# Threshold attention with an ELU feed-forward block: where SP's queue issues the loads of the next queries, of the tenth pair's values and of the next keys

## The chip, the cores and the metric

The kernel runs on one core of one Trainium2 chip. The metric is the device time of one execution in microseconds. Before the change, three runs took 1256.55, 1258.20 and 1259.09 us; the median is 1258.2 us.

## What is computed

```python
# q, k, v: (8 batches, 8 heads, 576 positions, 64); tau a number; all float32
scores = q @ k.transpose(0, 1, 3, 2) / 8
thresh = scores.max(-1, keepdims=True) - tau
scores = where(scores >= thresh, scores, -1e9)
scores = scores - scores.max(-1, keepdims=True)
attn = exp(scores); attn = attn / (attn.sum(-1, keepdims=True) + 1e-9)
y = attn @ v                                  # (8, 8, 576, 64)
x = y.transpose(0, 2, 1, 3).reshape(4608, 512)
h = x @ w_in                                  # w_in (512, 2048)
g = where(h > 0, h, exp(minimum(h, 0)) - 1)
out = g @ w_out                               # w_out (2048, 512), out (4608, 512)
```

## The kernel before

**Pairs.** Attention is worked off by pairs of heads, numbered from 0 to 31 (`NP`); four pairs make one batch. The code calls a pair `pr`, and its 576 positions are cut into four blocks of 128 and a rest of 64, the steps 0 to 3 and `NC`. The queries of a pair come in four DMAs of 72 KB into the buffer `qm`, the keys in four into `km`, the values in four (`vm` and `vd`, one of each for each head): `load` (L526) and `load_v` (L553). VectorE then transposes queries and keys in squares of 32 (`prep_q`, L577 to L579, and `prep_k`, L588 to L592); a scaling of the queries on POOL or ScalarE and a copy of keys follow.

**Two ways of ordering.** The first nine pairs are laid out by `early_tasks` (L1313): each step is a task with a time at which it is due, with corrections from the table `MOVED`, and with tasks that must come ahead of it; they are issued in the order of their times. From pair 9 on (`JOINED`, L1179), the tenth and the first *wide* one, a loop (L2133) writes out the order. It keeps a clock of its own, which each piece of TensorE work moves on, and an agenda: `at(t, f, key)` (L1673) puts f in at time t, moved by the table's entry for the stage and the key. The first wide pair has the stage "j", the others "s" and "f" in turn. These clocks only set in which order each engine's instructions are issued. On the chip every engine, and SP with its DMA issues, works its list in order and waits on semaphores. The DMAs of SP's queue take turns on eight semaphores, so that an issue also waits for the landing of the one eight before it.

**One wide pair.** `tail_step` (L1964) does the scores of the rest of 64 and the values of the pair two before. Then come two halves: `wide_step` (L1986) does the scores of two blocks for both heads, and maximum, exponential, mask, sum and reciprocal follow on VectorE, ScalarE and POOL. After each half's scores stand 14 quarters of feed-forward products on TensorE (`ffn_quarters`, L1930) for a batch that is done: either first products (`first_product`, L1703, seven products to a unit, the sums of blocks of w_in coming in by DMA as `sw`) or second rounds (`second_round`, L1834, with `t` coming in from `wout_sums`). The feed-forward products rotate through three banks of TensorE's result memory; a bank is written again when its readers have done, among them the adds of VectorE at L1746 and L1873. The two kinds fill pairs in turn: from pair 10 on, even pairs hold second rounds and odd pairs first products.

**The loads of a wide pair, before.** All go through SP. Seven microseconds (of the agenda's clock) after the pair's start come its own values (L2152), which the tail two pairs later reads. In the first half, behind `prep_q` of the next pair, come the next pair's keys (L2008); in the second half, behind `prep_k`, the queries of the pair after the next (L2006). Queries and keys share one buffer, `qm`, from here on (`shared`). So the queries of pair n+1 are issued in the second half of pair n-1, and `prep_q(n+1)` reads them in the first half of pair n. Between these loads SP issues the stores of the transposed weights (`there`, L886 and L898), their fetches (`wTa`, `wTb`, L906 and L910), the rests (`xtail`, L1072), the loads of sums (L1255, L1285) and the stores of results (L1148).

**The first wide pair, before.** The values of pair 9, the queries of pair 10 and the keys of pair 10 are loads of `early_tasks` (L1454 to L1462); the queries of pair 11 are loaded in pair 9's second half.

Of the kernel before, what the change touches and what calls it, by code (L numbers as in the profile page):

```python
# [368 lines left out]
def kernel(  # L369
# [806 lines left out]
    NP = B * NPAIR  # L1176
    NB = NC + 1
    per_seq = NPAIR * NB
    JOINED = (2 * NPAIR + 1)  # L1179
# [133 lines left out]
    def early_tasks():  # L1313
# [104 lines left out]
        for pr in range(1, NPAIR + 6):  # L1418
            old = ("sc", number[pr - 2, NC]) if pr > 1 else None
            own = pr < NPAIR  # L1420
            for x, name in enumerate("qk"):
                n = 2 * pr - 2 + x if own else number[pr - 1, 2 + x]
                k, late_ = kind(n), n >= LATE
                sooner = 2.0 * (n >= SWITCH)
                if pr in QK_PE:
                    tn = turned.setdefault(pr, {})

                    def run_turn(pr=pr, name=name, tn=tn):
                        room_for("t", lambda: do(("prep", name, pr)))
                        tn[name] = turn_blocks(pr, name)  # L1430

                    task(("turnqk", name, pr), begin[n] + (6.7 - sooner if late_ else 1.6), None, run_turn, ("load", name, pr))
                    task(("prep", name, pr), begin[n] + (6.8 - sooner if late_ else 1.7), f"p{name}{k}",
                         lambda pr=pr, name=name, tn=tn: copy_blocks(pr, name, tn[name]), ("turnqk", name, pr), None if own else old,
                         ("prep", "q", pr) if x else None)
                    if x:
                        def run_last(pr=pr, tn=tn):
                            room_for("t", lambda: do(("last", pr)))
                            tn["last"] = turn_last(pr)

                        task(("turnlast", pr), begin[n] + (6.7 - sooner if late_ else 1.6), None, run_last, ("load", "q", pr), ("load", "k", pr))
                        task(("last", pr), begin[n] + (6.8 - sooner if late_ else 1.7), None, lambda pr=pr, tn=tn: copy_last(pr, tn["last"]),
                             ("turnlast", pr), ("prep", "q", pr), ("prep", "k", pr))
                        made["scale", pr] = made["last", pr]
                else:
                    task(("prep", name, pr), begin[n] + (6.8 - sooner if late_ else 1.7), f"p{name}{k}",
                         lambda pr=pr, f=(prep_q, prep_k)[x]: f(pr), ("load", name, pr), None if own else old, ("prep", "q", pr) if x else None)
                if not x and pr not in QK_PE:
                    task(("scale", pr), begin[n] + (6.85 - sooner if late_ else 1.75), f"sq{k}", lambda pr=pr: scale_q(pr), ("prep", "q", pr))
                m = number[pr, 2] if own and not x else n  # L1450
                task(("copy", name, pr), begin[m] + (6.9 - sooner if late_ else 1.8), f"c{name}{kind(m)}",
                     lambda pr=pr, f=(copy_q, copy_k)[x]: f(pr), ("prep", name, pr), ("scale", pr) if not x or pr in QK_PE else None,
                     old if not x else None)
            for x, name in enumerate("qk"):  # L1454
                n = 2 * pr - 1 + x if own else number[pr - 1, 3 + x]
                late_ = n >= LATE
                task(("load", name, pr + 1), begin[n] + (7.0 if late_ else -1.0 if own else 4.6), f"l{name}{kind(n)}",
                     lambda pr=pr, name=name: load(pr + 1, (name + "m",)), ("prep", name, pr), ("last", pr) if pr in QK_PE else None)
            if pr > 1:
                n = 2 * pr - 3 if own else number[pr - 1, 3]  # L1460
                task(("v", pr), begin[n] + (7.1 if n >= LATE else 4.7), f"lv{kind(n)}", lambda pr=pr: load(pr, ("v",)),
                     ("load", "q", pr), None if own else ("val", pr - 2, 1))  # L1462
# [3 lines left out]
        for i, (n, x) in enumerate(slots):  # L1466
            late_, k, t = n >= LATE, f"{kind(n)}{x}", begin[n]
# [48 lines left out]
        for n in range(MIDDLE):  # L1516
            pr, i = steps[n]
# [143 lines left out]
    with tc.manual_schedule():  # L1661
# [11 lines left out]
        def at(t, f, key=None):  # L1673
            if key and stage[0]:
                t += MOVED.get(stage[0] + key, 0.0)
            serial[0] += 1
            heapq.heappush(agenda, (t, serial[0], f))
# [308 lines left out]
        def wide_step(pr, half):  # L1986
            t = clock[0]
            on_pe(2.15, lambda: wide_scores(pr, half))
            e = t + 2.15
            for s in range(2):  # L1990
                i = 2 * half + s
                at(e + 1.55 + 1.5 * s, lambda i=i: wide_bounds(pr, i), f"bound{i}")
                for h in range(2):
                    k = 2 * s + (h ^ s)
                    at(e + 0.75 * k, lambda i=i, h=h: wide_max(pr, i, h), f"max{i}{h}")
                    at(e + (1.6, 3.0, 4.7, 5.6)[k], lambda i=i, h=h: wide_exp(pr, i, h), f"exp{i}{h}")
                    at(e + (3.0, 4.3, 6.5, 6.9)[k], lambda i=i, h=h: wide_mask(pr, i, h), f"mask{i}{h}")
                finish_of(pr, i, e + (5.1, 7.8)[s], e + (8.4, 10.5)[s])
            if pr + 1 < NP:
                at(e + 5.2, lambda: (prep_k if half else prep_q)(pr + 1), f"prep{half}")  # L2000
                if not half:
                    at(e + 6.1, lambda: scale_q(pr + 1), "qscale")
                if half:
                    at(e + 6.1, lambda: copy_k(pr + 1), "kcopy")
                    if pr + 2 < NP:
                        at(e + 6.1, lambda: load(pr + 2, ("qm",), True), "loadq")  # L2006
                elif pr > JOINED:
                    at(e + 6.1, lambda: load(pr + 1, ("km",), True), "loadk")  # L2008
            extras(e + 0.3, e + 1.2, e + 4.2, e + 10.4, e + 12.0)
# [123 lines left out]
        for pr in range(JOINED, NP + 2):  # L2133
            t = clock[0]
            b = pr // NPAIR
            stage[:] = "j" if pr == JOINED else "sf"[pr % 2], BEFORE if pr == JOINED else 0, 0
            if pr == JOINED + 1:
                ges.append((raw.tile([P, S // T, T], FP32, name="km").rearrange("p j d -> p (j d)")[:, : 2 * CT], lambda: None))
            if pr == JOINED:
                for x, i in enumerate((NB - 2, NB - 1)):  # L2140
                    at(t + 6.0 + 3.0 * x, lambda pr=pr, i=i: fetch(pr - 1, i), f"fetch{x}")
                for x in range(3):
                    at(t + 7.0 + 6.0 * x, lambda x=x: nc.sync.dma_start(wout_sums[0, x], out_sums[x].rearrange("p u n -> p (u n)")), f"w{x}")
            elif pr <= NP:
                for x, i in enumerate((NC, 0, 1, 2, 3)):
                    at(t + 6.0 + 3.8 * x, lambda pr=pr, i=i: fetch(pr - 1, i), f"fetch{i}")
            if pr == NP:
                at(t + 12.0, split_begin)
                for x in range(8):
                    at(t + 1.0 + 1.9 * x, lambda: run_extra(max(0.9, extra[0][0])) if extra else None)  # L2150
            if JOINED < pr < NP:
                at(t + 7.0, lambda pr=pr: load(pr, ("v",)), "v" if stage[0] == "j" else None)  # L2152
            tail_step(pr)
            v_end = clock[0]
            if pr % NPAIR == 1 and pr < NP + 1:
                if b > 2:
                    xs = [late["first"].tile([P, 2, CT], FP32, name=f"x{x}") for x in range(3)]
                    jobs = sums_x(b - 1, xs)
                    at(t + 0.9, jobs[1])
                    for x, when in ((0, 0.6), (2, 1.3), (3, 4.0), (4, 4.7)):  # L2160
                        at(v_end + when, jobs[x])
                if pr > JOINED:
                    group(b - 1)
            if pr == NP + 1:
                break
            extras(t + 0.6, t + 2.8)
            begin, first_half = next(iter(SPLIT)) if pr == JOINED else (0, HALF_QUARTERS)
            ffn_quarters(begin - BEFORE if pr == JOINED else begin)
            for half in range(2):
                if pr < NP:  # L2170
                    wide_step(pr, half)
                ffn_quarters(2 * HALF_QUARTERS - begin - first_half if half else first_half)
# [225 lines left out]
```

## Time and profile before

| what | value |
|---|---|
| median of three runs | 1258.2 us |
| the profiled execution, its own time | 1257.49 us |
| its span, first to last instruction | 1255.7 us |
| granted TensorE clock, mean | 0.999 |
| TensorE matmuls busy | 1243.7 us, 99% |
| VectorE busy | 1039.8 us, 83% |
| POOL busy | 727.8 us, 58% |
| ScalarE busy | 635.4 us, 51% |
| DMA | 245.74 MB, mean 196 GB/s |
| DMA packets | 323871, of them under 512 B 207536 |

Busy times are of one execution, which the hardware profiler took down. An instruction's row has its start, its duration, engine, line of the kernel and the tiles that it writes and reads (out<-in). SPq rows are DMA issues: the duration is that of the issue, and the time to landing stands in another view. A busy TensorE is one with a matmul in flight.

### The profile page before, as it was taken

What the parts mean: (1) busy time and instruction counts of PE and PEld (TensorE: products, weight loads), DVE (VectorE), ACT (ScalarE), POOL (GpSimd) and SP (SyncE); (2) the same over time, 40 slices, a digit from 0 to 9 for tenths busy, and PEclk for the clock granted to TensorE, in tenths of its full rate; (3) what the DMA queues carried; (4) which work ended last, traced back from release to release, by engine and by line L of the source; (5) the groups of instructions that cost most, each with busy time, mean ns of one, the idle gap of its engine ahead of it and who ended that gap; (6) DMA issues with size and microseconds to landing.
All of it is one profiled execution on the core that took longest, in us unless ns stands there. A gap on an engine that the chain in (4) does not pass through costs nothing.

```text
span 1255.7 us, 21110 instructions
## 1 busy us (share of the span) xinstructions
PE 1243.7 (99%) x6596; PEld 956.7 (76%) x6596; DVE 1039.8 (83%) x2195; ACT 635.4 (51%) x1334; POOL 727.8 (58%) x1064
## 2 busy tenths in 40 slices
PE   8999999999999999999999999999999999999998
PEld 6675575477888787888778788878788887788886
DVE  7888777789898978998889889898889886776983
ACT  7899776664453526253534445352625352465330
POOL 5778655687575748676576747584767655122000
PEclk9999999999999999999999999999999999999999
DMA  7467788998989898898989988999889785000001
GB/s 150 147 172 184 171 246 228 262 271 219 237 227 257 245 253 230 231 254 227 259 208 244 245 234 227 253 252 248 230 224 268 221 242 174 20 1 1 1 34 34
DMA packets 323871, 245.74 MB, mean 196 GB/s; under 512 B 207536, under 2 KB 288304, under 8 KB 323760
## 3 DMA queue, kind: packets, MB, share of 16 engines
q1 hardware_dynamic: 322672, 243.71, 72.5%
q8 instruction: 52, 0.85, 0.3%
q10 hardware_dynamic: 1088, 0.69, 0.2%
q14 instruction: 59, 0.48, 0.1%
HBM read 154.53 MB, written 89.78 MB: 195 GB/s over the span
## 4 chain that ended last, share of the span: by engine, by line
PE 90%; DVE 3%; POOL 3%; DMA 2%; issue 1%; ACT 1%; SPq 1%; DVEq 0%; ACTq 0%; POOLq 0%
PE f L1864 23%; PE f L1724 21%; PE sc L982 7%; PE sc L1055 7%; PE f L2324 7%; PE f L2249 5%; PE f L1107 4%; PE sc L678 3%; PE f L1159 3%; PE f L2262 2%; PE pv L935 2%; PE rt L797 2%; PE sc L1047 1%; DMA there<-x 1%; PE sc L1042 1%
## 5 line engine op out<-in xcount | busy, mean ns | idle before, releaser
L989 DVE TENSOR_REDUCE mx<-sc 128x1 f32<-128x576 f32 x207 | 148.1, 749 | 29.7 <-PE sc L982 25.8
L731 POOL TENSOR_SCALAR w<-w,rs 128x576 f32<-128x576 f32 x144 | 115.8, 813 | 69.4 <-DVE rs L794 67.6
L1009 ACT ACTIVATE w<-sc,mx 128x576 f32<-128x576 f32 x113 | 81.4, 739 | 115.7 <-DVE mx L989 98.7
L873 DVE STREAM_TRANSPOSE x<-w 128x512 f32<-128x512 f32 (+1 forms) x153 | 108.9, 744 | 13.4 <-POOL w L731 11.7
L1001 POOL TENSOR_SCALAR th<-mx,ntau 128x2 f32<-128x2 f32 (+1 forms) x114 | 33.8, 297 | 134.0 <-DVE mx L989 134.0
L982 PE MATMUL sc<-kT,qT 64*128 64x448 f32 (+4 forms) x736 | 103.1, 416 | 0.3 <-ACT xs L1071 0.3
L982 PEld LDWEIGHTS sc<-kT,qT 64*128 64x128 f32 x736 | 80.7, 186 | 25.2 <-issue 16.2
L1016 DVE SCALAR_TENSOR_TENSOR w<-sc,th,w 128x576 f32<-128x576 f32 x113 | 88.2, 810 | 9.4 <-ACT w L1009 9.2
L1724 PE MATMUL f<-xt,sw 128*128 128x256 f32 x384 | 93.7, 386 | 1.5 <-DMA sw<-win_sums 0.9
L1864 PE MATMUL f<-w_out,s 128*128 128x256 f32 x384 | 92.0, 382 | 0.1
L1724 PE MATMUL f<-xt,w_in 128*128 128x256 f32 x384 | 92.0, 382 | 0.0
L1864 PE MATMUL f<-w_out,g 128*128 128x256 f32 x384 | 92.0, 382 | 0.0
L1724 PE MATMUL f<-x,w_in 128*128 128x256 f32 x384 | 90.9, 379 | 0.0
L1864 PE MATMUL f<-t,s 128*128 128x256 f32 x384 | 90.8, 379 | 0.0
L731 POOL TENSOR_SCALAR e<-e,rs 128x576 f32<-128x576 f32 x91 | 67.1, 741 | 35.3 <-DVE rs L794 34.0
L1724 PEld LDWEIGHTS f<-xt,sw 128*128 128x128 f32 x384 | 69.5, 189 | 18.4 <-issue 5.7
L1864 PEld LDWEIGHTS f<-w_out,g 128*128 128x128 f32 x384 | 72.0, 190 | 12.4 <-issue 3.1
L1864 PEld LDWEIGHTS f<-w_out,s 128*128 128x128 f32 x384 | 71.9, 190 | 12.4 <-issue 2.5
L1724 PEld LDWEIGHTS f<-xt,w_in 128*128 128x128 f32 x384 | 71.9, 190 | 12.3 <-ACT w L1738 1.5
L1724 PEld LDWEIGHTS f<-x,w_in 128*128 128x128 f32 x384 | 72.8, 190 | 10.5 <-ACT s L1738 0.7
L1864 PEld LDWEIGHTS f<-t,s 128*128 128x128 f32 x384 | 72.8, 190 | 10.3 <-POOL s L1811 0.4
L1811 POOL TENSOR_TENSOR s<-g 128x256 f32<-128x256 f32 x96 | 74.9, 785 | 8.0 <-DVE g L1774 7.4
(331 smaller groups left out, 3103.7 us busy)
## 6 DMA issues: line engine op xcount, KB each, us to landing
there<-x SPq DMA_DIRECT2D x444, 144.0 KB, 3.5
wTb<-there SPq DMA_DIRECT2D x58, 576.0 KB, 6.4
wTa<-there SPq DMA_DIRECT2D x53, 576.0 KB, 5.2
sw<-win_sums SPq DMA_DIRECT2D x46, 384.0 KB, 4.7
t<-wout_sums SPq DMA_DIRECT2D x33, 512.0 KB, 6.2
qm<-in_q_dram SPq DMA_DIRECT2D x124, 72.0 KB, 5.0
wst<-in_moe_w_in_dram SPq DMA_DIRECT2D x16, 512.0 KB, 4.5
vm<-in_v_dram SPq DMA_DIRECT2D x64, 128.0 KB, 3.7
```

Of the source, the lines that this page charges most:

```text
L731: nc.gpsimd.tensor_scalar(wv, wv, st["rs"][:, h : h + 1], 1.0, ALU.mult, ALU.mult)
L873: nc.vector.transpose(x[:, :, c0 : c0 + nc_], src.rearrange("p (c g n) -> p g c n", c=nc_, n=T))
L982: on_banks(nc.tensor.matmul(o, qT[r, i * P : (i + 1) * P], kT[r, k0 : k0 + n], start=True, stop=True, skip_group_check=True), o)
L989: on_banks(nc.vector.tensor_reduce(st["mx"][:, h : h + 1], st["sc", h], axis=AX.XY if i == NC else AX.X, op=ALU.max, negate=True), st["sc" ...
L1009: on_banks(nc.scalar.activation(st["e", h], st["sc", h], AF.Exp, bias=st["mx"][:, h : h + 1]), st["sc", h])
L1016: on_banks(nc.vector.scalar_tensor_tensor(st["e", h], st["sc", h], st["th"][:, h : h + 1], st["e", h], ALU.is_ge, ALU.mult, accum_out=st[" ...
L1055: on_banks(nc.tensor.matmul(o, vm[:, h, c], parts[part][:, g0:g1, h * (NC + 1) + c], start=False, stop=(c == NC - 1), skip_group_check=Tru ...
L1724: nc.tensor.matmul(loc["banks"][place], left[:, j], right[:, j], start=(begins and j == 0), stop=(j == 1), skip_group_check=True)
L1811: engine.tensor_tensor(o, x, y, op)
L1864: nc.tensor.matmul(place(m), lhs, rhs, start=(begins and v == 0), stop=(v == RU - 1), skip_group_check=True)
L2249: nc.tensor.matmul(o, w.rearrange("p (j f) -> p j f", j=KJ)[:, j], m, start=(j == 0 and x == 0), stop=(j == KJ - 1 and x == 1), skip_group ...
L2324: nc.tensor.matmul(banks8[2 * i + x // 2], h[:, tok], w, start=(f == 0 and x != 1), stop=(f == NFT - 1 and x != 0), skip_group_check=True)
```

## The change

Three things move; nothing is added or removed in what is computed or transferred.

- In wide pairs 10 to 30, the next pair's queries are loaded directly behind the pair's own values, seven microseconds after the pair's start on the agenda's clock. The load of queries in the second half goes.
- The values of pair 9 (the tenth) leave `early_tasks` and are loaded in the second half of pair 9, at the place (key "loadq") where the queries of pair 11 had been loaded.
- The keys of pair 10 leave `early_tasks` and are loaded 8.3 us after the start of pair 9.

```diff
@@ early_tasks
-            for x, name in enumerate("qk"):
+            for x, name in enumerate("qk" if pr < JOINED else "q"):
                 n = 2 * pr - 1 + x if own else number[pr - 1, 3 + x]
...
-            if pr > 1:
+            if 1 < pr < JOINED:
                 n = 2 * pr - 3 if own else number[pr - 1, 3]
                 task(("v", pr), begin[n] + (7.1 if n >= LATE else 4.7), f"lv{kind(n)}", lambda pr=pr: load(pr, ("v",)),
...
@@ wide_step
                 if half:
                     at(e + 6.1, lambda: copy_k(pr + 1), "kcopy")
-                    if pr + 2 < NP:
-                        at(e + 6.1, lambda: load(pr + 2, ("qm",), True), "loadq")
+                    if pr == JOINED:
+                        at(e + 6.1, lambda: load(pr, ("v",)), "loadq")
                 elif pr > JOINED:
                     at(e + 6.1, lambda: load(pr + 1, ("km",), True), "loadk")
@@ the loop over wide pairs
             if JOINED < pr < NP:
-                at(t + 7.0, lambda pr=pr: load(pr, ("v",)), "v" if stage[0] == "j" else None)
+                at(t + 7.0, lambda pr=pr: load(pr, ("v",)))
+                if pr + 1 < NP:
+                    at(t + 7.0, lambda pr=pr: load(pr + 1, ("qm",), True))
+            if pr == JOINED:
+                at(t + 8.3, lambda pr=pr: load(pr + 1, ("km",)))
```

## The prediction

> **What bounds the kernel now.** I read the page first, then the busy times of the stretch in which the wide pairs run, then who waited for whom on TensorE.
>
> ```profile
> span 1255.7 us, 21110 instructions
> PE 1243.7 (99%) x6596; PEld 956.7 (76%) x6596; DVE 1039.8 (83%) x2195; ACT 635.4 (51%) x1334; POOL 727.8 (58%) x1064
> ...
> 290.00:1006.00 716.00, 714.79 (x4008) 573.95 (x4007) 625.75 (x1380) 305.64 (x671) 468.48 (x704) 1.00 0.90 239
> ...
> PE f L1724 <- DMA sw<-win_sums: 0.9, 1, 0.9
> ...
> PE f L1724 <- DVE g L1746: 0.6, 1, 0.6
> ```
>
> The third row is the stretch of the wide pairs 10 to 30: of 716.00 us TensorE is busy 714.79, VectorE 625.75, the DMA engines 90%. The kernel is bound by TensorE, and nothing that only unloads another engine can give more than the waits that are left: 0.9 us for one late load of sums and 0.6 us for one late add (the other waits of TensorE lie in the first 62 us or are smaller). What can be lost has no such limit. So the question is what reaches TensorE when a load comes later.
>
> **The change, part by part.** Most of it is order on SP's queue; the order of instructions built from both kernels shows no other engine changed but for two neighbouring swaps ahead of the first wide pair.
>
> *The next queries.* Before, the four loads of q are issued in the second half of the pair before the one that transposes them. After, they stand behind the four loads of v of the very pair whose first half transposes them (prep_q, L579, on VectorE). The same four transfers, 21 pairs, moved past eight stores of x, the sums or output stores, xtail, two fetches and the v loads. In pair 13, seen before the change:
>
> ```profile
> 385.68 3.15 SPq L546 DMA_DIRECT2D qm<-in_q_dram  x4
> 389.79 5.42 SPq L898 DMA_DIRECT2D there<-x  x8
> ...
> 395.81 1.29 SPq L1285 DMA_DIRECT2D t<-wout_sums  x2
> ...
> 397.97 0.37 SPq L1072 DMA_DIRECT2D xtail<-xs  x1
> ...
> 400.15 0.51 SPq L560 DMA_DIRECT2D vm<-in_v_dram  x1
> ...
> 401.81 0.38 SPq L560 DMA_DIRECT2D vm<-in_v_dram  x1
> 403.46 0.47 SPq L562 DMA_DIRECT2D vd<-in_v_dram  x1
> 404.22 2.47 SPq L886 DMA_DIRECT2D there<-x  x4
> ...
> L562 SPq DMA_DIRECT2D vd<-in_v_dram x1: 471/471/471, 403.5 to 403.5; - x1
> ...
> DMA to landing us min/median/max: 3.2/3.2/3.2
> ```
>
> The last v load is issued at 403.46 and lands 3.2 later, at 406.66. The four q loads will follow it where the stores of L886 stand now, and one queue serves them in turn. What four cost behind others, I take from the neighbours in the same pair, four loads of k (the same size and shape) and the four L886 stores:
>
> ```profile
> L546 SPq DMA_DIRECT2D qm<-in_k_dram x4: 382/488/749, 407.3 to 408.8; - x4
> ...
> DMA to landing us min/median/max: 3.9/4.1/4.1
> L886 SPq DMA_DIRECT2D there<-x x4: 346/431/1133, 404.2 to 406.3; - x4
> ...
> DMA to landing us min/median/max: 1.9/2.6/2.8
> ```
>
> The k loads land from 407.3 + 3.9 = 411.2 to 408.8 + 4.1 = 412.9, 0.57 apart; the stores from 404.2 + 2.8 = 407.0 to 406.3 + 1.9 = 408.2, 0.4 apart. Four transfers: 1.6 to 2.3 us, and I take 1.9. So q is there at 406.66 + 1.9 = 408.6. Who needs it:
>
> ```profile
> 405.12 0.78 DVE L579 STREAM_TRANSPOSE qT<-qm 128x576 f32<-128x576 f32 x1
> ...
> 406.05 0.42 DVE L1746 TENSOR_TENSOR g<-f,t 128x256 f32<-128x256 f32 x1
> ...
> 405.78 1.89 PE L1724 MATMUL f<-xt,sw 128*128 128x256 f32 x8
> ```
>
> VectorE reaches prep_q at 405.12 and would stand there 3.4 us. Behind it in its queue come the sum, the reciprocal and the add of L1746, which reads a TensorE bank. That add ends at 406.05 + 0.42 = 406.47. The eight matmuls of the last row are two products, the second of them starts half-way, at 405.78 + 0.86 = 406.64, and writes the bank that the add has read. Only 0.17 us of cover. So the stall of VectorE passes to TensorE nearly whole: 3.4 - 0.17 = **3.3 us** in this pair, and TensorE has no idle time later in which to make it up.
>
> How many pairs are like it? The odd pairs (11 to 29, ten of them) run first products in this place, the even ones second rounds. Among the odd ones, five (13, 17, 21, 25, 29) reach the v loads late, behind the loads of t; the last of them and two of the other five, the best and the worst:
>
> ```profile
> L562 SPq DMA_DIRECT2D vd<-in_v_dram x1: 471/471/471, 950.1 to 950.1; - x1
> ...
> DMA to landing us min/median/max: 3.0/3.0/3.0
> 951.05 0.78 DVE L579 STREAM_TRANSPOSE qT<-qm 128x576 f32<-128x576 f32 x1
> L562 SPq DMA_DIRECT2D vd<-in_v_dram x1: 515/515/515, 467.8 to 467.8; - x1
> ...
> DMA to landing us min/median/max: 3.4/3.4/3.4
> 473.24 0.77 DVE L579 STREAM_TRANSPOSE qT<-qm 128x576 f32<-128x576 f32 x1
> L562 SPq DMA_DIRECT2D vd<-in_v_dram x1: 471/471/471, 606.1 to 606.1; - x1
> ...
> DMA to landing us min/median/max: 5.0/5.0/5.0
> 610.48 0.77 DVE L579 STREAM_TRANSPOSE qT<-qm 128x576 f32<-128x576 f32 x1
> ```
>
> Pair 29: 950.1 + 3.0 + 1.9 - 951.05 - 0.17 = 3.8. Pair 15: 467.8 + 3.4 + 1.9 = 473.1, just ahead of 473.24, no stall. Pair 19: 606.1 + 5.0 + 1.9 - 610.48 - 0.17 = 2.35. As they stand, five at the mean of 3.3 and 3.8 and five at the mean of 0 and 2.35 make 17.8 + 5.9 = 23.7 us. But the q loads that leave the end of the pair before also leave the queue that makes pairs 19 and 29 later than their kind. I choose: the late five at pair 13's 3.3 (there VectorE's data and not q held the stores: q is issued by 388.83, the stores wait until 389.79), the others at half of 5.9. That gives 16.5 + 2.9 = **19.4 us**.
>
> The even pairs have more cover. In the tightest, pair 22:
>
> ```profile
> L562 SPq DMA_DIRECT2D vd<-in_v_dram x1: 514/514/514, 709.7 to 709.7; - x1
> ...
> DMA to landing us min/median/max: 2.2/2.2/2.2
> 713.35 0.78 DVE L579 STREAM_TRANSPOSE qT<-qm 128x576 f32<-128x576 f32 x1
> 716.53 0.40 DVE L1873 TENSOR_TENSOR t<-f,s 128x256 f32<-128x256 f32 x1
> 717.68 1.89 PE L1864 MATMUL f<-t,s 128*128 128x256 f32 x8
> ```
>
> q lands at 709.7 + 2.2 + 1.9 = 713.8, 0.45 after prep_q's time; the add that TensorE waits for ends at 716.93, 0.75 ahead of its matmul, and VectorE idles in between as well. Cost nothing; without that cover up to 0.5 in one pair.
>
> *What q pushes back.* L886, the sums load, k and the fetches come some 2 us later on SP. k lands at 412.9 in pair 13 and its transpose runs at 419.55:
>
> ```profile
> 419.55 0.77 DVE L592 STREAM_TRANSPOSE kT<-qm 128x576 f32<-128x576 f32 x1
> ```
>
> so 6.6 us cover 2. The q scaling behind prep_q waits on POOL or ACT in order; POOL is busy 468 of 716 us and its queue moves with TensorE's stall, so I add nothing. The second half loses four issues on SP; I credit the one wait of 0.9 us there (it is in pair 17, which stalls earlier in any case).
>
> *The first wide pair.* The v loads of the tenth pair take the place of four q loads in its second half, and are read two pairs later. The next keys go behind L886, ahead of the sums; up to eight issues ahead of them are gone. Nothing to nothing: at best the 0.6 us wait of L1746 goes, at worst it doubles. I take 0.
>
> Sum: 19.4 - 0.9 = **+18.5 us**. The profiled execution took 1257.5 (span 1255.7 and 1.8 around it), 0.7 below the median of 1258.2: 1276.0 on its own time, 1276.5 to 1277 beside the median. I say 1276.5.
>
> *The clock.* The granted clock is 1.00 through the whole stretch, whose longest wait of TensorE is 0.9 us; no row shows a stall of 3 us. The Trainium skill ("TensorE: Matmul & The Clock Gate", "What's actually happening") says that the clock falls to half after an idle window of about 3.4 us, which runs freely, and comes back after a busy one. By that page most stalls here would be too short to hold a whole window, and the sum stays; what it would be otherwise is the second rival.
>
> **The rivals.**
>
> *Not slower.* With four issues fewer at each pair's end, SP could reach the v loads as early as in pair 15, 5.4 us before prep_q, in all pairs. Then q lands in time everywhere, the two waits of 0.9 and 0.6 go, and the time is 1258.2 - 1.5 = 1256.7. It decides when the last v load of the late five is issued 3.5 us sooner. Against it: in pair 13 nearly 1 us of waiting lies between the old q loads and the stores, so SP was not held by them. 8%.
>
> *A colder clock.* If stalls of 3.3 us drop the clock to half for as long again, each of the late five costs 1.7 us more: 1276.5 + 8.5 = 1285. For it: the stalls are long; against it: the clock row above, though without such a stall. 10%.
>
> *The even pairs stall too.* If q takes 1 us longer than 1.9 (each issue of the k loads took up to 0.75 us), the eleven even pairs lose up to 0.7 each and the odd ones 1 more in at least five: 1276.5 + 12 = 1288. 10%.
>
> **How the numbers follow.** My forecast has the remaining 72%. With four transfers at 1.6 it is 5 x 3.0 + 0 - 1.5 = +13.5, 1271.5; at 2.3, without any relief, five at 3.95 and five at 1.5, +27, 1285. The range reaches towards the rivals, 1265 to 1288. About 0.2% (2.5 us) is what a measurement of this kernel can tell from no change. Faster 4% and same 4%, the two halves of the first rival; slower 92%.
>
> **What would show it.** In the profile after: VectorE idle ahead of L579, released by the q load, some 3 us in pairs 13, 17, 21, 25, 29 and little in the others; TensorE idle ahead of L1724, released by L1746, by nearly the same time; busy time of TensorE unchanged. Wrong would be: q landing ahead of prep_q in the late five, VectorE waiting with TensorE not waiting, or TensorE busy for longer.

## The result and the profile after

The changed kernel takes 1281.62 us (median of four runs, 1280.91 to 1281.81); the kernel before, run beside it, 1258.64 us (1256.55 to 1259.79). The ratio is 1.0184 with a 95% interval of 1.0171 to 1.0196: about 23 us slower, 5 us more than the predicted 1276.5 and inside its range.

The page of the profile after begins like this.

```profile
span 1279.9 us, 21131 instructions
PE 1254.1 (98%) x6596; PEld 961.2 (75%) x6596; DVE 1041.6 (81%) x2195; ACT 636.0 (50%) x1334; POOL 729.9 (57%) x1064
```

The span is 24.2 us longer, and TensorE is busy for 10.4 us longer with the same 6596 matmuls. So stalls alone are not the answer: something made matmuls slower too. The stretch of the wide pairs, by engine (busy time and instructions of TensorE, its weight loads, VectorE, ScalarE, POOL; then granted clock, DMA share, GB/s):

```profile
295.00:1030.00 735.00, 722.94 (x4005) 577.85 (x4002) 626.85 (x1380) 305.69 (x671) 469.34 (x703) 0.99 0.85 232
```

TensorE is idle for 12.1 us of 735, where it had been idle for 1.2 of 716, and the clock is no longer 1.00. The waits of TensorE (total, times, longest) name the idle time:

```profile
PE f L1724 <- DVE g L1746: 12.2, 8, 2.8
PE sc L678 <- DVE w L780: 2.4, 1, 2.4
PE sc L1042 <- ACT w L758: 0.5, 1, 0.5
```

The first row is the predicted wait. The old wait of 0.9 us for sums is gone. The other two rows are new, lie ahead of the first wide pair and at its first scores, and were not predicted.

**One late pair.** SP's queue in pair 13, which starts at 397.8, and the four q loads with their time to landing:

```profile
407.76 0.48 SPq L562 DMA_DIRECT2D vd<-in_v_dram  x1
408.49 2.00 SPq L546 DMA_DIRECT2D qm<-in_q_dram  x4
410.59 2.90 SPq L886 DMA_DIRECT2D there<-x  x4
```

```profile
L546 SPq DMA_DIRECT2D qm<-in_q_dram x4: 377/496/500, 408.5 to 410.0; - x4
...
  DVE qT L579: 3.0, 1
...
DMA to landing us min/median/max: 3.5/3.8/3.9
```

The last load of q is issued at 410.0 and lands some 3.5 us later, at 413.5. VectorE:

```profile
413.73 0.78 DVE L579 STREAM_TRANSPOSE qT<-qm 128x576 f32<-128x576 f32 x1 [3.01 <-DMA qm<-in_q_dram]
414.44 0.11 DVE L788 TENSOR_REDUCE su<-sm 128x2 f32<-128x4 f32 x1
414.58 0.17 DVE L794 RECIPROCAL rs<-su 128x2 f32<-128x2 f32 x1
414.67 0.42 DVE L1746 TENSOR_TENSOR g<-f,t 128x256 f32<-128x256 f32 x1
```

It stands 3.01 us ahead of prep_q, and the add of L1746 comes three instructions later. TensorE waits for that add:

```profile
415.14 1.13 PE L1724 MATMUL f<-xt,sw 128*128 128x256 f32 x4 [2.82 <-DVE g L1746]
...
417.56 3.00 PE L1724 MATMUL f<-xt,w_in 128*128 128x256 f32 x8
420.39 1.89 PE L1724 MATMUL f<-x,w_in 128*128 128x256 f32 x8
```

2.82 of the 3.01 us get through: the cover is 0.19. The second row is the surprise. Eight such matmuls take 1.89 us, as in the third row, and here they took 3.00: the stall is over, and TensorE is slow.

**The other odd pairs.** VectorE at prep_q in pairs 15, 17, 19 and 29, then TensorE's waits in pairs 17, 21, 25 and 29:

```profile
483.53 0.78 DVE L579 STREAM_TRANSPOSE qT<-qm 128x576 f32<-128x576 f32 x1
...
554.05 0.78 DVE L579 STREAM_TRANSPOSE qT<-qm 128x576 f32<-128x576 f32 x1 [2.30 <-DMA qm<-in_q_dram]
...
624.04 0.78 DVE L579 STREAM_TRANSPOSE qT<-qm 128x576 f32<-128x576 f32 x1
...
973.83 0.78 DVE L579 STREAM_TRANSPOSE qT<-qm 128x576 f32<-128x576 f32 x1 [2.33 <-DMA qm<-in_q_dram]
```

```profile
555.46 0.92 PE L1724 MATMUL f<-xt,sw 128*128 128x256 f32 x3 [2.12 <-DVE g L1746]
...
695.87 1.73 PE L1724 MATMUL f<-xt,sw 128*128 128x256 f32 x4 [2.04 <-DVE g L1746]
...
836.16 1.13 PE L1724 MATMUL f<-xt,sw 128*128 128x256 f32 x4 [1.95 <-DVE g L1746]
...
975.24 1.21 PE L1724 MATMUL f<-xt,sw 128*128 128x256 f32 x4 [2.14 <-DVE g L1746]
```

The five late pairs are the five named ahead; for pairs 15 and 19 the view shows no wait. From one pair's first L1042 matmul to the next one's, pair 13 went from 34.10 to 38.87 us, 17 from 35.12 to 38.17 (its old sums wait is in the 35.12), 21 from 34.13 to 38.09, 25 from 34.10 to 36.32 and 29 from 34.34 to 38.20. Even pairs from 12 on keep 34.01. Pair 25 lost 2.2 us after a stall of 1.95, and the other four, after stalls of 2.04 to 2.82, lost 3.9 to 4.8 (pair 17 without its old wait of 0.87: 38.17 - 34.25).

**The clock.** The records of the granted clock show it at half in four stretches of 3.41 us, from 416.37, 556.32, 696.27 and 976.16. These starts lie 41, 41 and 82 times 3.413 us apart. So I laid windows of 3.413 us on that grid; each pair of rows is the window of a stall and the one behind it, in pairs 13, 25 and 29 (second number of a row: its length; third: TensorE's busy time; third from the end: the granted clock).

```profile
412.96:416.37 3.41, 1.23 (x6) 1.10 (x7) 2.60 (x8) 0.86 (x3) 1.51 (x3) 1.00 0.82 197
416.37:419.78 3.41, 3.41 (x10) 2.69 (x9) 3.34 (x8) 1.02 (x4) 3.41 (x5) 0.50 0.92 164
...
832.81:836.22 3.41, 1.46 (x8) 0.96 (x6) 1.43 (x5) 0.64 (x1) 0.38 (x2) 1.00 0.91 157
836.22:839.63 3.41, 3.41 (x16) 3.02 (x17) 3.34 (x10) 1.97 (x5) 3.41 (x6) 1.00 0.96 197
972.75:976.16 3.41, 1.27 (x6) 0.84 (x5) 2.30 (x6) 0.55 (x2) 1.21 (x2) 1.00 0.82 202
976.16:979.57 3.41, 3.41 (x9) 2.72 (x9) 3.34 (x9) 1.08 (x4) 3.41 (x6) 0.50 0.89 168
```

A window in which TensorE is busy for 1.23 or 1.27 of 3.41 us is followed by one at half clock (10 and 9 matmuls run in it); after 1.46 the clock stays and 16 run. In pairs 17 and 21 it is 1.29 and 1.37, with half clock behind. Half the clock for 3.41 us loses 1.7 us, four times 6.8 (an estimate: it takes TensorE as bound by its clock all through the window).

**Ahead of the first wide pair.** TensorE before, and after:

```profile
250.06 0.81 PE L930 MATMUL pv<-wTb,vd 128*128 128x384 f32 x2
250.79 2.37 PE L935 MATMUL pv<-wTb,vm 128*64 128x320 f32 x16
253.10 1.24 PE L678 MATMUL sc<-kT,qd 128*128 128x288 f32 x4
```

```profile
253.77 1.21 PE L678 MATMUL sc<-kT,qd 128*128 128x288 f32 x4 [2.44 <-DVE w L780]
254.82 0.81 PE L930 MATMUL pv<-wTb,vd 128*128 128x384 f32 x2
255.56 2.38 PE L935 MATMUL pv<-wTb,vm 128*64 128x320 f32 x16
```

The values of pair 7 (L930, L935) and the last scores of pair 8 (L678) have changed places. Before, the values filled the time in which VectorE did the mask of L780 for which the scores wait; after, TensorE stands for 2.44 us and then does the same work.

Pair by pair, the 24.2 us of span are 4.8 up to the start of pair 9 (0.9 of it is there at 46 us, ahead of anything that the change touches) and 19.4 in pairs 9 to 30. The end behind them is as long as before.

### The profile page after: what moved, and what is told of

Read it like the earlier page. It is cut to its first block, busy times and chain, and to the rows that moved or that the text cites. A ratio compares the mean times of both kernels' runs of the same rounds, so it can differ in the third digit from the quotient of the medians.

```text
span 1279.9 us, 21131 instructions
## 1 busy us (share of the span) xinstructions
PE 1254.1 (98%) x6596; PEld 961.2 (75%) x6596; DVE 1041.6 (81%) x2195; ACT 636.0 (50%) x1334; POOL 729.9 (57%) x1064
## 4 chain that ended last, share of the span: by engine, by line
PE 82%; DMA 7%; DVE 5%; ACT 2%; SPq 2%; issue 1%; POOL 1%; DVEq 0%; ACTq 0%; POOLq 0%
PE f L1864 21%; PE f L1724 19%; PE f L2328 7%; PE sc L982 7%; PE sc L1055 5%; PE f L2253 5%; PE f L1107 4%; PE sc L678 3%; PE f L1159 3%; DMA out_dram<-ot 3%; PE f L2266 2%; PE pv L935 2%; PE rt L797 2%; DMA qm<-in_q_dram 2%; DVE x L873 1%
## 5 line engine op out<-in xcount | busy, mean ns | idle before, releaser
L1724 PE MATMUL f<-xt,sw 128*128 128x256 f32 x384 | 96.5, 390 | 12.2 <-DVE g L1746 12.2
L1724 PE MATMUL f<-xt,w_in 128*128 128x256 f32 x384 | 95.3, 392 | 0.0
L1724 PEld LDWEIGHTS f<-xt,sw 128*128 128x128 f32 x384 | 69.6, 190 | 30.9 <-DVE g L1746 16.3
```

What stands on the lines that cost most here:

```text
L1724: nc.tensor.matmul(loc["banks"][place], left[:, j], right[:, j], start=(begins and j == 0), stop=(j == 1), skip_group_check=True)
```

## The experiments

My theory: late q holds VectorE, that holds TensorE in five pairs, the stalls drop the clock, and apart from these the swap at the join costs some 3 us. The rivals: the clock or the swap is not a cause of its own; the stores, sums and keys pushed back by q cost as much as q; the order of q and v decides. In all ratios the divisor is the kernel before, run beside the experiment (medians 1258.7, 1259.16 and 1258.18 us in the three groups of runs). A diff is against the changed kernel where nothing else is said.

### Half of the change each: q_only and join_only

q_only is the kernel before with the queries' load moved alone; join_only the kernel before with pair 9's values and pair 10's keys moved alone.

The edit of q_only, against the kernel before (that of join_only is the rest of the change's diff):

```diff
-                    if pr + 2 < NP:
-                        at(e + 6.1, lambda: load(pr + 2, ("qm",), True), "loadq")
...
-                at(t + 7.0, lambda pr=pr: load(pr, ("v",)), "v" if stage[0] == "j" else None)
+                at(t + 7.0, lambda pr=pr: load(pr, ("v",)))
+                if pr + 1 < NP:
+                    at(t + 7.0, lambda pr=pr: load(pr + 1, ("qm",), True))
```

> Only the queries' loads of wide pairs 10 to 30 are moved behind the values; the tenth pair's values and the next keys stay where they were before. Theory (the transpose of queries waits for their landing, the add behind it on VectorE is late, TensorE stalls, mostly in the pairs 13, 17, 21, 25, 29): the pairs from 9 to 30 grew by 19.4 us together in the changed kernel and this does the same, 1258.6 + 19.4 = 1278. Rival (the loss needs both parts, since the first wide pair sets how far SP's queue is behind in all later pairs): under 1270.

Measured: 1276.46 us, ratio 1.0137 (1.0117 to 1.0156). The waits of TensorE:

```profile
PE f L1724 <- DVE g L1746: 12.1, 6, 2.7
```

> Only the tenth pair's values and the next keys are moved; the queries are loaded in the second half as before. Theory (without the task that loads the tenth pair's values nothing pulls the last values of pair 7 ahead of the last scores of pair 8 any more, so TensorE stands at these scores for VectorE's mask, 2.4 us, and 0.5 us at the first wide scores): plus 3 to 4 us, 1262. Rival (the start of the kernel differs by 0.9 us anyhow, and the join costs nothing that repeats): 1258.6.

Measured: 1261.7 us, ratio 1.0022 (1.0014 to 1.0031). Its wait at L678 is again 2.4 us; but here nearly the whole stall, 2.30 us, lies in one window, and the clock falls behind it:

```profile
250.43:253.84 3.41, 1.11 (x5) 0.93 (x6) 3.08 (x8) 0.95 (x2) 2.72 (x6) 1.00 0.84 242
253.84:257.25 3.41, 3.41 (x11) 1.22 (x11) 1.66 (x3) 0.00 (x0) 0.00 (x0) 0.50 1.02 319
```

In the changed kernel the same 2.44 us stall falls across two windows, each busy for 2.2 us, and the clock stays:

```profile
249.13:252.54 3.41, 2.21 (x10) 0.94 (x8) 2.96 (x6) 2.87 (x6) 1.96 (x6) 1.00 0.95 225
252.54:255.95 3.41, 2.18 (x10) 1.33 (x12) 2.91 (x10) 0.00 (x0) 1.79 (x3) 1.00 0.69 205
```

What follows: both halves cost time, the queries some 17 us and the join some 3. Together that is 20 of the 23. On top of the late queries the join costs more than alone: the changed kernel is 5.9 us above q_only by the ratios, and three more comparisons of versions further down that differ in the join or its swap alone (val_pulled, t_later and prep_later) give 5.2 to 5.9. Part of that lies in pair 11, which takes 34.10 us in q_only and 34.11 in join_only, and 34.94 with both. What is left is of the size by which runs of one version differ, since each stall's clock drop (1.7 us) hangs on where its windows lie.

The mean granted clock of each execution shows how much that is. Of the four of q_only the fastest, 1273.34 us, ran at 0.999 and the slowest, 1279.71, at 0.993: 6.4 us apart, where 0.006 of 1275 us is 7.7. The changed kernel has 0.995 or 0.996 in all four, the kernel before 0.999 in its profile.

### The swap alone: val_pulled

A task of `early_tasks` may pull others ahead. The removed task of pair 9's values had to come behind the last values of pair 7 and pulled them forward. val_pulled keeps that task in the changed kernel, but without a load in it. The two pieces of TensorE change back; the loads stay where the change put them.

```diff
-            if 1 < pr < JOINED:
+            if pr > 1:
...
-                task(("v", pr), begin[n] + (7.1 if n >= LATE else 4.7), f"lv{kind(n)}", lambda pr=pr: load(pr, ("v",)),
+                task(("v", pr), begin[n] + (7.1 if n >= LATE else 4.7), f"lv{kind(n)}", lambda pr=pr: load(pr, ("v",)) if pr < JOINED else None,
```

> The changed kernel, with the task of the tenth pair's values kept at its time as a task that does nothing but pull the last values of pair 7 ahead, as before; all loads as in the changed kernel. Only the two swapped pieces on TensorE go back. Theory: 3 to 4 us faster than the changed kernel, 1278. Rival (the later keys and values themselves, or the transpose of keys that changed places on VectorE, made the wait): 1281.6.

Measured: 1275.44 us (1274.94 to 1279.95), ratio 1.0137 (1.0118 to 1.0155), against 1.0184 with the swap. The wait of 2.44 us is gone, and those behind L1746 are all there (14.6 us in seven; the profile is of the slowest execution). That is some 6 us less than the changed kernel, where 3 to 4 were expected. What follows: the order of these two pieces is nearly all that the join costs. The moved loads of pairs 9 and 10 show in one place: pair 11 still takes 34.77 us here, with a wait behind L1746, as in the changed kernel. Why they reach as far as pair 11 is not shown.

### The five late pairs alone: five_as_before

```diff
+                    if pr + 1 in (13, 17, 21, 25, 29):
+                        at(e + 6.1, lambda: load(pr + 2, ("qm",), True), "loadq")
...
-                if pr + 1 < NP:
+                if pr + 1 < NP and pr not in (13, 17, 21, 25, 29):
```

> The changed kernel, with the queries that are transposed in the pairs 13, 17, 21, 25 and 29 loaded a half earlier as before, and those of the other sixteen behind the values. Theory: the five pairs' growth of 17.9 us goes, 1263 to 1264, and TensorE's waits at L1724 on L1746 go with it in these five. Rival (four DMA issues more in any pair's first half push the stores, sums and fetches and cost everywhere): a quarter of the 19.4 goes, 1277.

Measured: 1263.65 us, ratio 1.0038 (1.0023 to 1.0053).

```profile
PE sc L678 <- DVE w L780: 2.4, 1, 2.4
PE f L1724 <- DVE g L1746: 1.2, 3, 0.6
```

The five pairs are back at 34.10 us with q loaded early in them alone. The other sixteen late loads together cost the 1.2 us of waits in the second row, or 1.8 us by the lengths of the pairs, half of it in pair 11; the rest of what is left is the join, with a clock drop behind its stall in this profile. So nearly all of the queries' loss lies in these five pairs, and what q pushes back on SP in the others costs at most these 1.8 us.

### The queries ahead of the values: q_ahead_of_v

```diff
-                at(t + 7.0, lambda pr=pr: load(pr, ("v",)))
                 if pr + 1 < NP:
                     at(t + 7.0, lambda pr=pr: load(pr + 1, ("qm",), True))
+                at(t + 7.0, lambda pr=pr: load(pr, ("v",)))
```

> The changed kernel with the two groups of loads in turn: the next queries first, the pair's own values behind them, both at the same place of SP's queue. Theory: queries land some 2 us sooner, 13 to 13.5 us after the pair's start, against 12.8 at which the transpose is due; five stalls of 0.3 to 0.5 us at most, no stall long enough for the clock to fall, 1258.6 + 3 + 2 = 1264. Rival (two groups of loads side by side in one place make the loss, in whatever order): 1281.

Measured: 1271.92 us, ratio 1.0104 (1.0091 to 1.0117). A miss: it got back less than half of the loss. SP in pair 13, and TensorE's waits:

```profile
407.12 5.04 SPq L546 DMA_DIRECT2D qm<-in_q_dram  x4
```

```profile
PE f L1724 <- DVE g L1746: 5.9, 6, 1.6
```

The four q issues took 5.04 us instead of 2.00. The third starts at 408.95 and its row lasts 2.41 us; the fourth starts at 411.42. The DMAs eight ahead of these two are the two loads of t (L1285), issued at 403.2 and 403.9, which took 5.7 and 7.5 us to land, to 408.9 and 411.4. Each of the two q issues starts just when the load of t eight ahead of it has landed, so it is for these landings that SP waits here. What is shown besides: not the v loads but what stands ahead of both keeps q back in these pairs.

### That which stands ahead: t_later, t_later_join_before, t_later_before

The late five are the odd pairs in which the loads of t, two half-megabyte blocks, go out early in the pair. In the changed kernel's pair 13:

```profile
400.39 1.34 SPq L1285 DMA_DIRECT2D t<-wout_sums  x2
...
DMA to landing us min/median/max: 5.7/6.1/6.6
```

The second is issued at 401.1 and lands 6.6 us later, at 407.7. The last v load stands eight behind it and starts at 407.76; SP has nothing in hand in the microsecond ahead of that, and the q loads follow.

t_later issues the two loads of t 16 us later, behind the sums and fetches of the first half; t_later_join_before is the same on q_only, without the join's part; t_later_before the same on the kernel before.

```diff
-    (0.65, lambda: round2("w1", 1, LO)), (0.15, lambda: next_t(2)),
+    (0.65, lambda: round2("w1", 1, LO)), (16.0 if r else 0.15, lambda: next_t(2)),
...
-    (0.2, lambda: final(1, HI, 5, "t5")), (0.15, lambda: next_t(1)),
+    (0.2, lambda: final(1, HI, 5, "t5")), (16.0 if r else 0.15, lambda: next_t(1)),
```

> The changed kernel with two of the three loads of t that stand ahead of xtail and the values in the pairs 13, 17, 21, 25 and 29 issued 16 us later on the agenda, behind the first half's sums load and fetches. Theory (these five stall because the two half-megabyte loads of t hold up values and queries): queries land about 12.5 us after the pair's start as in the other odd pairs, the five stalls and the drops of the clock go, 1264, with the join's 3 us left. Rival (the transfers of the first half are too many in whatever order; the late thing is then the sums load, as in the run with the later transpose): a wait of TensorE for sums in its place, 1270 or more.

Measured: 1265.47 us, ratio 1.0052 (1.0036 to 1.0069). The waits of TensorE:

```profile
PE f L1724 <- DVE g L1746: 2.5, 4, 0.9
```

In pair 13 the last v load goes out 7.9 us into the pair instead of 9.9. q lands in time, and all five pairs take 34.10 us again, with q still behind v.

> The same with the tenth pair's values and the next keys as before the change. Theory: 1260 to 1261, no loss but some tenths of a microsecond in the odd pairs; a gain over the kernel before only if its wait of 0.9 us for sums goes and nothing comes in its place. Rival: 1267 or more.

Measured: 1259.87 us, ratio 1.0011 (1.0002 to 1.0020). With the join as before, next to nothing of the change's cost is left.

> The kernel before the change with nothing but the two loads of t moved in the same way: what this edit does by itself. Theory: TensorE waited for no load of t or sums but once for 0.9 us, so nothing to gain but that: 1258 to 1259. Rival (the two loads ahead of a sums load make it late): 1262 or more.

Measured: 1257.80 us, ratio 0.9998 (0.9989 to 1.0007). The loads of t may come later at no cost, and gain nothing by themselves. What follows: the late q needs both, the move behind v and the loads of t ahead of it. The eight semaphores are one way in which t reaches q; the bytes of t, which go ahead of q's on the same queue, are another, and no run parts the two.

### The transpose later: prep_later, prep_later_join_before, prep_later_keys_behind

If VectorE's order is the fault, prep_q may go behind the adds of L1746. prep_later moves prep_q, the scaling and the next keys' load 2.6 us back on the agenda. On SP the keys thereby go behind the two fetches of L906 (in pair 13: the fetches from 413.03, the keys from 414.53). prep_later_join_before is the same on q_only. The edit of prep_later:

```diff
-                at(e + 5.2, lambda: (prep_k if half else prep_q)(pr + 1), f"prep{half}")
+                at(e + 5.2 + (2.6 if not half and pr > JOINED else 0.0), lambda: (prep_k if half else prep_q)(pr + 1), f"prep{half}")
...
-                    at(e + 6.1, lambda: scale_q(pr + 1), "qscale")
+                    at(e + 6.1 + (2.6 if pr > JOINED else 0.0), lambda: scale_q(pr + 1), "qscale")
...
-                    at(e + 6.1, lambda: load(pr + 1, ("km",), True), "loadk")
+                    at(e + 6.1 + 2.6, lambda: load(pr + 1, ("km",), True), "loadk")
```

> The changed kernel with the transpose of the next queries, their scaling and the load of the next keys put 2.6 us later on the agenda: in the odd pairs the transpose then comes behind the two adds and the two masks on VectorE, some 3.5 us later than before, and no load is moved. Theory: the queries (landed 15 to 15.7 us after the pair's start at worst) are there at 16.4, TensorE no longer waits, 1258.6 + 3 = 1262. Rival (it is the loads' being on the queue at that place, not VectorE's place of waiting, that costs): 1278 to 1282.

Measured: 1272.06 us, ratio 1.0102 (1.0086 to 1.0118).

```profile
PE f L1724 <- DMA sw<-win_sums: 9.1, 4, 3.1
...
PE f L1724 <- ACT ge L1754: 2.2, 1, 2.2
PE f L1724 <- DVE g L1746: 0.7, 2, 0.4
```

The wait at L1746 is gone, as it should be, and one for the sums stands in its place. In pair 13 the second load of sums is issued at 422.71, and TensorE, after a wait of 3.13 us, goes on at 427.77. Four stores of L898 stand just ahead of that load on SP and take 4.33 us; what holds them there is not shown.

> The queries behind the values and the transpose 2.6 us later as in the run of that edit, and the tenth pair's values and the next keys as before the change. Theory: both losses are gone, the four issues at the second half's end stay gone and with them the 0.9 us wait for sums: 1257.8, the same as before or 0.1% faster. Rival (a remainder of the queue's load stays): 1260 to 1264.

Measured: 1265.29 us, ratio 1.0057 (1.0041 to 1.0072). A miss again, with smaller waits for sums (3.0 us in four).

> The run with the later transpose, with the load of the next keys put behind the second sums load of the pair (no longer ahead of it). In that run VectorE no longer waited for queries, but TensorE waited up to 3.1 us for the sums load, which SP issued some 4 us later than before, behind four issues of keys that took up to 1.2 us each. Theory (SP's queue is what is late now, and the next thing in it passes the wait on): the waits for sums go, 1262 to 1264. Rival (DMA volume, not order): 1270 or more.

Its edit is that of prep_later, but for the keys, which go behind the second load of sums:

```diff
-                    at(e + 6.1, lambda: load(pr + 1, ("km",), True), "loadk")
+                    at(e + 10.0, lambda: load(pr + 1, ("km",), True))
```

Measured: 1279.55 us, ratio 1.0167 (1.0152 to 1.0182). A miss. The waits of TensorE, those of VectorE, and VectorE in pair 13:

```profile
PE f L1724 <- DVE g L1746: 13.7, 11, 2.5
```

```profile
DVE kT L592 <- DMA qm<-in_k_dram: 14.7, 10, 2.7
```

```profile
428.66 0.78 DVE L592 STREAM_TRANSPOSE kT<-qm 128x576 f32<-128x576 f32 x1 [1.05 <-DMA qm<-in_k_dram]
```

The sums come in time, the keys don't: VectorE now stands ahead of prep_k (L592), with the same add behind it. All three fit one reading: SP's order in the late pairs has no room of its own, and whichever of q, sums and keys goes last of those due is the one waited for. It is argued from these waits and not tried further.

### The clock alone: kept_busy

In the five late pairs the first product of the second unit is computed three times into the same bank, with the same result. TensorE then has 40 matmuls more (8.6 us, since eight begin within 1.73), placed where it would stand idle.

```diff
-                for j in range(2):
+                again = 3 if k == 0 and r == 0 and v == 1 and g > 1 else 1
+                for j in tuple(range(2)) * again:
```

> The changed kernel with the first product of the second unit done three times over instead of once in each of the five late pairs, with the same result: 1.7 us more of TensorE work directly ahead of the product that waits. Theory (the clock falls to half for 3.4 us after these stalls and so costs 1.7 us each time, four or five times): the added work fills the stall, the clock stays at 1.00, and the kernel is 6 to 8 us faster than the changed kernel, 1274, though it does 8.6 us more work. Rival (the clock's record tells nothing, the matmuls behind the stall are slow for other reasons): as the changed kernel or up to 2 us slower, 1281 to 1284.

Measured: 1278.35 us, ratio 1.0153 (1.0140 to 1.0167), against 1.0184 for the changed kernel: less time with more work. The stall's window of pair 13 and the next (the lines of the kernel are one higher here):

```profile
412.79:416.20 3.41, 2.33 (x12) 1.73 (x10) 1.45 (x5) 0.00 (x0) 0.35 (x1) 1.00 0.55 115
416.20:419.61 3.41, 3.41 (x16) 3.03 (x17) 3.34 (x10) 1.97 (x5) 3.41 (x6) 1.00 1.04 198
```

```profile
PE f L1725 <- DVE g L1747: 5.5, 8, 1.1
```

No clock drop is left in the five pairs; VectorE waits for q no less than in the changed kernel (16.1 us in eleven waits, there 14.8 in ten). The gain is smaller than the 6 to 8 us expected: 5.5 us of waits are left, and in this execution the join's stall fell into one window and cost a drop of its own. The terms are -6.7 (idle time, from 12.2 to 5.5), -6.8 (four drops), +1.7 (that one) and +8.6 (work): -3.2, and 1278.35 - 1281.62 is -3.3.

## Why the prediction was right in its cause and 5 us short

- **q lands after VectorE is due, and the stall passes to TensorE.** Right, in the five pairs named, with 0.56 us in pair 11 and 0.17 in pair 27 beside them. Of the 3.01 us of VectorE in pair 13, 2.82 reach TensorE: a cover of 0.19 against 0.17 predicted. In pairs 17 to 29 the difference is 0.18 to 0.19 as well. five_as_before shows that these pairs hold the loss, t_later that what makes q late there is the loads of t ahead of it.
- **3.3 us in each of the late five, 16.5.** Too much. Pair 13 stalls 2.82, the others 1.95 to 2.14, together 11.1. The relief that I had granted the other five pairs alone worked here too: with four q issues fewer at the end of the pair before, the first v load leaves 6.5 to 6.9 us after the pair's start and not 7.8 to 9.1. q lands 15.7 us into pair 13 where my sum gave 16.3.
- **2.9 us in the other odd pairs.** The two waits just named and a few tenths of longer busy time: 1.65 us by the pairs' lengths. Of the right kind, at the lower end.
- **Even pairs nothing, the sums' wait of 0.9 gone, k and the sums covered.** Right: the even pairs from 12 on keep 34.01 us, and the row of that wait is gone from the profile. But little of the cover of the sums and keys is left: prep_later and prep_later_keys_behind were held by them.
- **The clock, priced at nothing.** This is the step that failed. I took the rule of the Trainium skill ("TensorE: Matmul & The Clock Gate", "What's actually happening") to need an idle window of 3.4 us, and put the drop at 10% as a rival. The Trainium skill's free-running window is borne out: half-clock stretches of 3.41 us on one grid. But the window doesn't have to be wholly idle. In the profiles of both kernels and of all twelve experiments I put TensorE's idle time into windows of the grid (from 200 us on): all 18 drops follow a window with 1.90 us or more of idle time, and the longest without a drop is 1.95. The bound lies at some 1.9 to 2.0 of 3.41. The stalls of the late five lie just over it. The rival's price of 1.7 us each was right, its condition of 3.3 us was not: four of five, 6.8 us.
- **The first wide pair, priced at nothing.** Wrong by 3 us and more: 2.44 + 0.18 + 0.50 of new waits there, and more than that by the ratios. I had the "two neighbouring swaps" in view and gave them no price. The place held no spare work: before, 3.0 us of values on TensorE covered VectorE's mask. val_pulled shows that the swap alone brings the 2.44.

So +16.5 + 2.9 - 0.9 + 0 + 0 became, in the profile, +11.1 (idle) +0.8 (longer busy time around the five stalls), +1.65, -0.9, +6.8 (clock), +3.1 and +0.8 (join), and +0.9 that was there ahead of all of it: 24.3, against 24.2 of span. The forecast was this near by luck: a term too large stood against two left out. "Busy time of TensorE unchanged", which the prediction named as a sign, was false; "TensorE busy for longer", which it named as a sign of being wrong, came true with 10.4 us, and this is what pointed at the clock.

The rival "not slower" fell for the late five only: in the others SP was early enough, as it said, and t_later makes it true for all. "Even pairs stall too" fell altogether.

What stays open: what the join costs on top of the late queries beyond its new waits, what holds the stores of L898 in prep_later, and where the clock's windows lie in other executions than the profiled ones, of which the mean clock alone is known. No version is measurably faster than the kernel before; t_later_before comes out even with it.

## What to carry to other kernels

Ahead of a load that is moved to just before its use, look at what stands behind the *reader* in its engine's queue: here a transpose that waits for a DMA held up an add that frees a TensorE bank, with 0.2 us to spare. Price a TensorE stall at its length plus the clock, if it can fill more than half of a 3.4 us window (here some 1.9 us). And when a task goes from a list that is ordered by due times and dependencies, compare the orders of each engine, since the task may have pulled something else forward.

## What the runs showed of the hardware

- A stall of 2.0 us of TensorE can halve its clock for 3.41 us. Whether it does hangs on where it lies in the grid of windows: the join's 2.44 us cost no drop where it was cut into 1.24 and 1.20, and one where 2.30 of it lay in a single window.
- Work without use, put in a stall, can shorten the time: 8.6 us more of matmuls and 3 us less in all.
- What SP's issues take depends on what is still in flight: four issues of q took 2.00, 2.21 and 5.04 us in pair 13 of three versions, and the 5.04 us held the landing of two loads of t, 5.7 and 7.5 us after their issue.
